# Splitting transposed head pairs in gapped half copies on VectorE, with the preparation of two pairs in a new order

## The chip, the cores and the metric

The kernel runs on one core of a Trainium2 chip. The metric is the device time of one execution in microseconds; the kernel before has a median of 217.63 us over 7 runs. Engines are named as in the profile: PE is TensorE, DVE is VectorE, ACT is ScalarE, POOL is GpSimd, SP is the queue that issues nearly all DMAs.

## The reference

Block-sparse attention for 4 batches of 8 heads, 768 positions, head width 64, followed by a gated block:

```python
scores = (1.0 / np.sqrt(D)) * np.matmul(q, k.transpose(0, 1, 3, 2))
scores = np.where(mask, scores, -1e9)           # mask: neighbours, first and last block, 3 drawn blocks of 32
attn = np.exp(scores - max); attn = attn / (attn.sum(-1) + 1e-9)
x = (attn @ v) with heads side by side           # (4, 768, 512)
h = np.maximum(x @ w_in, 0.0); u, v = h[..., :512], h[..., 512:]
v_n = (v - mean(v)) / np.sqrt(var(v) + 1e-6)     # over the last axis
v_s = einsum('ts,bsd->btd', w_spatial, v_n) + b_spatial[None, :, None]
out = (u * v_s) @ w_out
```

Inputs and output are float32; the kernel computes its products in bfloat16.

## The kernel before

The 32 heads are worked in 16 pairs, four pairs to a batch. A head's scores are computed with the keys on the partitions, in six chunks of 128 keys. For one chunk, `qk_exp` (L356) multiplies a chunk of k with all 768 queries (two products of 384 columns, L361), and ScalarE takes the exponential of the 128x768 result (L365). One such chunk is a *slot*; a pair takes 12 slots, s = 0 to 11, and g = 12p + s counts them through. The mask is part of the product: below the 64 rows of k and q stand 24 rows with block indicators and penalties. Seven slots later `av` (L370) multiplies the exponentials with v, which has a column of ones so that the row sums come along; `norm` (L436) divides (rc L442, xn L443), and `xtr` (L459) transposes the result of a pair by DMA into xt. The first batch (pairs 0 to 3) runs through the same steps in halves of 384 queries (`qk_exp_half` L386, `av_half` L405, `xtr_half` L427 with its evacuation L434), over 48 values of g.

For pairs 4 to 15, k and q come to their place in five steps: `load` (L105) issues three DMAs on SP (L110) into staging tiles with two buffers per name; `prepare` (L147) casts k, q and v to bfloat16 on GpSimd (L140 and L143); `tr_dma` (L342) transposes k and q of both heads by DMA (L344) into tt_k and tt_q, 128 partitions by six chunks of 128 columns; `split_pair` (L347) copies the upper and the lower 64 partitions of tt into the two heads' own tiles with two VectorE copies of 64x768 (L350), one call for k and one for q. The split of pair p + 1 has to be done before the slot s = 0 of that pair.

The gated block of a batch is a list of steps made by `moe_units` (L487), one product of 128x512 in each (L520), and the slots of the following batch take them from a queue, one a slot at first and about two later. A v part is evacuated by VectorE (vsb L533), followed by statistics (L536, L537); after each three v parts GpSimd computes rstd (L540, L542), and VectorE normalises (vn L547). The spatial products follow (gn L586), transposed by DMA on SP (gt L590), then the output products, evacuated by ScalarE (L608) or VectorE (L610). These products share two PSUM banks, `moe0` and `moe1`, one buffer each, so that a product can start only when the one before the last has been evacuated.

The order of everything is the order of the program text: each engine works through its own queue in that order. The slots at which `load`, `prepare`, `tr_dma` and `split_pair` are called are written out by hand in the loop over p and s from L728 on; what is called earlier in the text stands earlier in the queues of all engines that it uses.

Of the kernel before, what the change touches and what calls it, by code (L numbers as in the profile page):

```python
# [11 lines left out]
BF16 = mybir.dt.bfloat16  # L12
# [14 lines left out]
def kernel(  # L27
# [16 lines left out]
    nc = tc.nc  # L44

    B, H, S, D = q.shape
# [3 lines left out]
    NCH = S // 128  # L50
# [6 lines left out]
    NG = H // 2  # L57
# [282 lines left out]
    tt = {}  # L340

    def tr_dma(p, nm):  # L342
        tt[nm, p] = work.tile([128, NCH, 128], BF16, tag=f"tt_{nm}", bufs=2, name=f"tt_{nm}")
        nc.sync.dma_start_transpose(out=tt[nm, p],  # L344
                                    in_=nat.pop((nm, p)).rearrange("p c h d -> p (c h d)"))

    def split_pair(p, nm):  # L347
        src = tt.pop((nm, p)).rearrange("x c n -> x (c n)")
        for h in range(2):
            nc.vector.tensor_copy(out=(qt if nm == "q" else kt)[(2 * p + h) % H][0:D, :],  # L350
                                  in_=src[h * D:(h + 1) * D, :])


    a_ref, av_ref, xn_ref, xt_ref = {}, {}, {}, {}
# [317 lines left out]
    for g in range(N0):  # L672
        qk_exp_half(g)
        if g < 6:
            keep_warm(2)
        if g == 12:
            mask_product(1, bank([128, 512], FP32), dve_copy)
        if g == 0:
            qt_mask(1, 2, 0)
        if g == 1:  # L680
            tr_k_head(1, 0, NCH)
            cast_qk(1, "k", slice(0, 1), nc.vector)
            qt_mask(2, 4, 0)
        for p, third in tr_slots.get(g, ()):
            tr_pair(p, "k", third)
        if g in q_slots:
            tr_q_pair(*q_slots[g])
        if g == 13:
            for p in range(2):
                cast_q_pair(p, 1)  # L690
            qt_mask(4, 8, 1, nc.gpsimd)
            cast_q_pair(2, 1)
            cast_weights(2)
            cast_q_pair(3, 1)
            cast_weights(2)
            prepare(4, "kq")
            load_weights(3)
        if g in (6, 20):
            qt_mask(*{6: (4, 8, 0), 20: (1, 4, 1)}[g])
        if g == 26:  # L700
            moe_q.extend(moe_units(0))
        if g == 28:
            tr_dma(4, "k")
            tr_dma(4, "q")
            cast_weights(2)
            load(4, "v")
            load(5, "kqv")
            wspt(0)
            wspt(1)
            cast_weights(1)  # L710
            prepare(5, "kq")
            wspt(2)
            wspt(3)
            tr_dma(5, "k")
            tr_dma(5, "q")
            wspt(4)
            wspt(5)
            load(6)
        if g in (36, 42):
            cast_v(4 if g == 36 else 5)  # L720
        if g in (39, 45):
            split_pair(4, "k" if g == 39 else "q")
        first_batch_rest(g)
        if g >= 26 and g != 32:
            moe_q.popleft()()
        first_batch_x(g)

    for p in range(NG, NP + 1):  # L728
        for s in range(12):
            g = 12 * p + s  # L730
            change = NG < p < NP and p % NG == 0
            j, ci = divmod(g, NCH)
            if p == NP and g - LAG >= 2 * NP * NCH:
                break
            if p < NP:
                qk_exp(j, ci)
            if p + 1 < NP and s in ((3, 6) if p == NG else (7, 10)):
                split_pair(p + 1, "k" if s in (3, 7) else "q")
            if s == (10 if p == NG else 8 if change else 6) and p + 2 < NP:
                tr_dma(p + 2, "k")  # L740
                tr_dma(p + 2, "q")
            if s == (7 if p == NG else 1) and p + 2 < NP:
                prepare(p + 2)
                if p == 6:
                    cast_weights(2)
            if s == (9 if change else 7) and p + 2 < NP:
                if p + 3 < NP:
                    load(p + 3)
                if p == 5:
                    load_weights(2)  # L750
            if g < N0 + 11 and g != N0 + 8:
                moe_q.popleft()()
            if g == N0 + 11:
                slots_left = 49
            if moe_q and slots_left > 0:
                budget += len(moe_q) / slots_left
                slots_left -= 1
                while moe_q and budget >= 0.5:
                    moe_q.popleft()()
                    budget -= 1  # L760
            first_batch_rest(g)
            first_batch_x(g)
            if g >= N0 + LAG:
                ja, qc = divmod(g - LAG, NCH)
                av(ja, qc)
                if qc == NCH - 1:
                    norm(ja)
            if s == (6 if change else 8) and p > NG:
                xtr(p - 1)
            if s == 11 and change:  # L770
                moe_q.extend(moe_units(p // NG - 1))
                slots_left = 48 if p < NP - NG else 49
                budget = 0.0
# [34 lines left out]
```

## Time and profile before

| | |
|---|---|
| median of 7 runs | 217.63 us (216.16 to 219.61) |
| the profiled execution's own time | 217.57 us |
| its span | 215.8 us |
| TensorE busy | 206.1 us (95%) |
| ScalarE busy | 172.4 us (80%) |
| VectorE busy | 131.0 us (61%) |
| GpSimd busy | 69.6 us (32%) |
| TensorE clock granted, mean | 0.997 |

The profile is of one execution. Times in its views are microseconds from the span's start, durations of single instructions are nanoseconds in the list of groups and microseconds in the timeline. A line of the list of groups has the line of the kernel, the engine, the operation, what it writes and reads, the shapes and the count; then the busy time in all and the mean of one; then how long the engine stood idle just before these instructions, and what ended that. A line of the timeline has start, duration and the same names; in square brackets is the idle time ahead of it and what ended it. A line of the list of waits says who waited for whom, for how long in all, how often, and the longest.

### The profile page before, as it was taken

To read this page: it belongs to the slowest core of one execution; us is meant where nothing else is said; L and a number is where in the kernel's file an instruction comes from. 1 tells how busy PE (TensorE), PEld (TensorE's weight loads), DVE (VectorE), ACT (ScalarE), POOL (GpSimd) and SP (SyncE) were. 2 spreads that over 40 slices of the span, in tenths; PEclk is the share of its full clock that TensorE was granted. 3 is DMA by queue.
4 is the path that set the end of the run, shared out by engine and by line. 5 is a ranking of instruction groups with operands and counts; after the bars stand their busy time and mean duration, and the time that the engine had idled before them with its cause. 6 is when DMAs were issued, how large, how long until landed. Compare 5 with 4: busy or idle time off the path is not lost.

```text
span 215.8 us, 5234 instructions
## 1 busy us (share of the span) xinstructions
PE 206.1 (95%) x2065; PEld 125.9 (58%) x2099; DVE 131.0 (61%) x311; ACT 172.4 (80%) x238; POOL 69.6 (32%) x97
## 2 busy tenths in 40 slices
PE   8999999999979999999999999999899999999993
PEld 7667766566646666655566565655555655544441
DVE  6776949967554546356957464445978344585542
ACT  7799999999988999998899888888789885266031
POOL 7678979802626121403242400401502000022000
PEclk9999999999999999999999999999999999999998
DMA  6999999998999899999989138979702124620246
GB/s 175 282 328 382 392 346 281 211 140 260 269 254 265 135 242 181 269 293 309 189 206 255 40 71 228 259 166 303 151 12 39 24 52 87 220 101 0 59 119 235
DMA packets 64936, 42.24 MB, mean 196 GB/s; under 512 B 46896, under 2 KB 60560, under 8 KB 64912
## 3 DMA queue, kind: packets, MB, share of 16 engines
q1 hardware_dynamic: 64624, 41.58, 77.0%
q8 instruction: 16, 0.26, 0.5%
q10 hardware_dynamic: 288, 0.33, 0.5%
q14 instruction: 8, 0.07, 0.1%
HBM read 24.38 MB, written 6.29 MB: 142 GB/s over the span
## 4 chain that ended last, share of the span: by engine, by line
PE 75%; DMA 7%; DVE 5%; SPq 4%; POOL 3%; issue 3%; ACT 0%; POOLq 0%; ACTq 0%; DVEq 0%
PE ps_moe L520 30%; PE ps L361 17%; PE ps_av L377 11%; DMA st_v<-in_v_dram 6%; PE ps L396 6%; PE ps_av L412 3%; PE ps_t L520 3%; PE ps_sc L520 3%; SPq L110 1%; POOL vv L143 1%; SPq L472 1%; DVE kt_all L350 1%; DVE vsb L533 1%; DMA out_dram<-osb 1%; POOL rstd L542 1%
## 5 line engine op out<-in xcount | busy, mean ns | idle before, releaser
L365 ACT ACTIVATE a_all<-ps 128x768 bf16<-128x768 f32 x144 | 113.5, 813 | 15.9 <-PE ps L361 9.6
L361 PE MATMUL ps<-qt_all,kt_all 88*128 88x384 bf16 x288 | 70.3, 325 | 1.1 <-DVE qt_all L350 1.1
L377 PEld LDWEIGHTS <-a_all 128*128 128x128 bf16 x864 | 46.1, 97 | 34.0 <-issue 1.6
L377 PE MATMUL ps_av<-vv,a_all 128*128 128x65 bf16 x864 | 50.8, 194 | 0.3
L520 PE MATMUL ps_moe<-w_in_t,xt 128*128 128x512 bf16 x143 | 45.2, 378 | 1.8 <-DVE vsb L533 0.8
L400 ACT ACTIVATE a_all<-ps 128x768 bf16<-128x768 f32 x48 | 35.6, 812 | 2.8 <-PE ps L396 2.3
L140 POOL CAST nat_k<-st_k 128x768 bf16<-128x768 f32 (+1 forms) x14 | 11.1, 790 | 71.9 <-DMA st_k<-in_k_dram 62.5
L520 PE MATMUL ps_moe<-vn,w_spt 128*128 128x512 bf16 x110 | 33.1, 378 | 0.3
L586 DVE SCALAR_TENSOR_TENSOR gn<-ps_moe,b_col,un 128x512 bf16<-128x512 f32 x20 | 15.0, 749 | 21.4 <-PE ps_moe L520 17.9
L520 PEld LDWEIGHTS <-xt 128*128 128x128 bf16 x192 | 18.6, 97 | 15.1 <-issue 0.8
L396 PE MATMUL ps<-qt_all,kt_all 88*128 88x384 bf16 x96 | 23.6, 327 | 0.7 <-ACT a_all L400 0.2
L520 PE MATMUL ps_moe<-w_out_t,gt 128*128 128x512 bf16 x73 | 21.5, 378 | 0.3
L520 PEld LDWEIGHTS <-w_spt 128*128 128x128 bf16 x144 | 13.8, 97 | 11.6
L361 PEld LDWEIGHTS <-kt_all 88*128 88x128 bf16 x288 | 19.0, 98 | 1.6 <-DVE qt_all L350 1.2
L412 PEld LDWEIGHTS <-a_all 128*128 128x128 bf16 x288 | 14.9, 98 | 6.3 <-issue 0.9
L533 DVE TENSOR_SCALAR vsb<-ps_moe 128x512 bf16<-128x512 f32 x18 | 12.3, 682 | 10.0 <-PE ps_moe L520 9.8
L536 DVE BATCH_NORM_STATS2 stats<-vsb 128x6 f32<-128x512 bf16 x24 | 16.6, 693 | 1.5 <-ACT vsb L531 0.8
L412 PE MATMUL ps_av<-vv,a_all 128*128 128x65 bf16 x288 | 17.1, 194 | 0.4 <-DVE xt L434 0.4
L540 POOL TENSOR_SCALAR std<-mv 128x3 f32<-128x3 f32 x8 | 1.9, 244 | 43.1 <-DVE mv L537 30.6
L610 DVE COPY osb<-ps_moe 128x512 f32<-128x512 f32 x10 | 6.9, 690 | 13.3 <-PE ps_moe L520 9.8
L443 DVE TENSOR_TENSOR xn<-ps_av,rc 128x384 bf16<-128x384 f32 x24 | 13.4, 557 | 0.8
L520 PEld LDWEIGHTS <-gt 128*128 128x128 bf16 x96 | 8.8, 97 | 7.1
(100 smaller groups left out, 212.8 us busy)
## 6 DMA issues: line engine op xcount, KB each, us to landing
out_dram<-osb SPq DMA_DIRECT2D x23, 256.0 KB, 3.3
st_v<-in_v_dram SPq DMA_DIRECT2D x14, 384.0 KB, 5.3
st_k<-in_k_dram SPq DMA_DIRECT2D x13, 384.0 KB, 4.3
st_q<-in_q_dram SPq DMA_DIRECT2D x12, 384.0 KB, 3.6
wst<-in_moe_w_spatial_dram SPq DMA_DIRECT2D x3, 768.0 KB, 9.1
wst<-in_moe_w_in_dram SPq DMA_DIRECT2D x4, 512.0 KB, 7.5
wst<-in_moe_w_out_dram SPq DMA_DIRECT2D x2, 512.0 KB, 6.6
st_q<-in_q_dram SPq DMA_DIRECT2D x4, 192.0 KB, 6.1
```

The source lines that it names most:

```text
L140: eng.tensor_copy(out=dst, in_=src)
L361: nc.tensor.matmul(out=ps[:, hf * 512:hf * 512 + HALF], lhsT=kt[j % H][:, ci * 128:(ci + 1) * 128], rhs=qt[j % H][:, hf * HALF:(hf + 1) * ...
L365: nc.scalar.activation(out=a_ref[j][:, ci, :].rearrange("p (b c) -> p b c", b=2), in_=ps.rearrange("p (b c) -> p b c", b=2)[:, :, 0:HALF], ...
L377: nc.tensor.matmul(out=av_ref[j][:, qc, :], lhsT=a_ref[j][:, ci, qc * 128:(qc + 1) * 128], rhs=vv[p % NG][:, h, ci, :], start=(ci == 0), s ...
L396: nc.tensor.matmul(out=ps[:, u * 512:u * 512 + HALF], lhsT=kt[j][:, ci * 128:(ci + 1) * 128], rhs=qt[j][:, grp * HALF:(grp + 1) * HALF], s ...
L400: nc.scalar.activation(out=a_ref["half", gh][:, 2 * i:2 * i + 2, :], in_=ps.rearrange("p (b c) -> p b c", b=2)[:, :, 0:HALF], func=AF.Exp, ...
L412: nc.tensor.matmul(out=av_ref["half", gh][:, qc, :], lhsT=a_ref["half", gh][:, ci, qc * 128:(qc + 1) * 128], rhs=vv[p][:, h, ci, :], start ...
L443: nc.vector.tensor_tensor(out=xn_ref[p][:, :, h, :], in0=ps[:, :, 0:D], in1=rc.to_broadcast([128, NCH, D]), op=ALU.mult)
L520: nc.tensor.matmul(out=box[0], lhsT=lhs, rhs=rhs, start=(i == 0), stop=(i == n - 1))
L533: nc.vector.tensor_scalar(out=vsb[:, tcc, :], in0=ps, scalar1=0.0, scalar2=None, op0=ALU.max)
L536: nc.vector.bn_stats(out=stats, in_=vsb[:, tcc, :])
L586: nc.vector.scalar_tensor_tensor(out=gn[:, tcc, :], in0=ps, scalar=b_col[:, tcc:tcc + 1], in1=un[:, tcc, :], op0=ALU.add, op1=ALU.mult)
```

## The change

`tr_dma` makes tt with 144 columns per chunk and uses the first 128, so that the chunks lie 16 columns apart. `split_pair` copies three chunks at a time: each of its copies of 64x768 becomes two of 64x384, with a source of three pieces and a destination without gaps.

The slots change for some pairs. The v cast of pair 5 moves from g = 42 to p = 4, s = 5 (g = 53), the q split of pair 4 from g = 45 to g = 44. In the slots of pair 4, the load of pair 7 moves from s = 7 to s = 11, behind the transposes of pair 6. In those of pair 5, pair 6 is split at s = 6 and 8 instead of 7 and 10, pair 7 is prepared at s = 7 instead of 1 and transposed at s = 9 instead of 6, and the load of pair 8 with the last two weight loads moves from s = 7 to s = 10. In those of pair 7, the load of pair 10 moves from s = 7 to s = 10. Within a slot, `prepare` now stands ahead of `tr_dma`.

```diff
     def tr_dma(p, nm):
-        tt[nm, p] = work.tile([128, NCH, 128], BF16, tag=f"tt_{nm}", bufs=2, name=f"tt_{nm}")
+        tt[nm, p] = work.tile([128, NCH, 144], BF16, tag=f"tt_{nm}", bufs=2,
+                              name=f"tt_{nm}")[:, :, 0:128]
         nc.sync.dma_start_transpose(out=tt[nm, p],
                                     in_=nat.pop((nm, p)).rearrange("p c h d -> p (c h d)"))
 
     def split_pair(p, nm):
-        src = tt.pop((nm, p)).rearrange("x c n -> x (c n)")
+        src = tt.pop((nm, p))
         for h in range(2):
-            nc.vector.tensor_copy(out=(qt if nm == "q" else kt)[(2 * p + h) % H][0:D, :],
-                                  in_=src[h * D:(h + 1) * D, :])
+            dst = (qt if nm == "q" else kt)[(2 * p + h) % H]
+            for c in (0, 3):
+                nc.vector.tensor_copy(out=dst[0:D, c * 128:(c + 3) * 128],
+                                      in_=src[h * D:(h + 1) * D, c:c + 3, :])
...
-        if g in (36, 42):
-            cast_v(4 if g == 36 else 5)
-        if g in (39, 45):
+        if g == 36:
+            cast_v(4)
+        if g in (39, 44):
             split_pair(4, "k" if g == 39 else "q")
...
     for p in range(NG, NP + 1):
+        change = NG < p < NP and p % NG == 0
+        splits = {NG: (3, 6), NG + 1: (6, 8)}.get(p, (7, 10))
+        s_prep = {NG: 7, NG + 1: 7}.get(p, 1)
+        s_tr = {NG: 10, NG + 1: 9}.get(p, 8 if change else 6)
+        s_load = {NG: 11, NG + 1: 10, NG + 3: 10}.get(p, 9 if change else 7)
...
-            if p + 1 < NP and s in ((3, 6) if p == NG else (7, 10)):
-                split_pair(p + 1, "k" if s in (3, 7) else "q")
-            if s == (10 if p == NG else 8 if change else 6) and p + 2 < NP:
+            if p + 1 < NP and s in splits:
+                split_pair(p + 1, "k" if s == splits[0] else "q")
+            if p == NG and s == 5:
+                cast_v(5)
+            if s == s_prep and p + 2 < NP:
+                prepare(p + 2)
+                if p == NG + 2:
+                    cast_weights(2)
+            if s == s_tr and p + 2 < NP:
                 tr_dma(p + 2, "k")
                 tr_dma(p + 2, "q")
-            if s == (7 if p == NG else 1) and p + 2 < NP:
-                prepare(p + 2)
-                if p == 6:
-                    cast_weights(2)
-            if s == (9 if change else 7) and p + 2 < NP:
-                if p + 3 < NP:
-                    load(p + 3)
-                if p == 5:
+            if s == s_load and p + 3 < NP:
+                load(p + 3)
+                if p == NG + 1:
                     load_weights(2)
```

## The prediction, made before the change was run

> **What bounds the kernel now.** I read the page's first part, then the list of what TensorE waited for, then the timelines of VectorE and GpSimd around each such wait.
>
> ```profile
> PE 206.1 (95%) x2065; PEld 125.9 (58%) x2099; DVE 131.0 (61%) x311; ACT 172.4 (80%) x238; POOL 69.6 (32%) x97
> ```
>
> TensorE is busy for 206.1 of 215.8 us, and that work is untouched. Only its idle time can be recovered, and only a new wait of TensorE can be lost. VectorE has 85 us free in total, but it works in order: what matters is whether a copy stands ahead of something that TensorE needs. TensorE's waits from 36 to 66 us, then from 66 to 180 us (time in all, number, longest):
>
> ```profile
> PE ps L361 <- DVE qt_all L350: 1.1, 1, 1.1
> PE ps_av L412 <- DVE xt L434: 0.4, 1, 0.4
> PE ps_moe L520 <- DVE vsb L533: 0.3, 1, 0.3
> ...
> PE ps_moe L520 <- DVE vsb L533: 0.6, 1, 0.6
> PE ps_moe L520 <- DVE osb L610: 0.3, 1, 0.3
> ```
>
> That is 2.7 us of named waits over the stretch in which pairs are split. The largest is pair 6's first product, held by the q split. The VectorE timeline, then GpSimd's:
>
> ```profile
> 57.83 0.18 DVE L537 BATCH_NORM_AGGREGATE mv<-stats 128x2 f32<-128x6 f32 x1
> 60.78 0.41 DVE L547 TENSOR_SCALAR vn<-vsb,mv,rstd 128x512 bf16<-128x512 bf16 x1 [2.77 <-POOL rstd L542]
> 61.11 0.19 DVE L442 RECIPROCAL rc<-ps_av 128x6 f32<-128x6 f32 x1
> 61.34 0.56 DVE L443 TENSOR_TENSOR xn<-ps_av,rc 128x384 bf16<-128x384 f32 x1
> 61.81 0.73 DVE L350 COPY kt_all<-tt_k 64x768 bf16<-64x768 bf16 x2
> 62.56 0.74 DVE L547 TENSOR_SCALAR vn<-vsb,mv,rstd 128x512 bf16<-128x512 bf16 x2
> 63.21 0.73 DVE L350 COPY qt_all<-tt_q 64x768 bf16<-64x768 bf16 x2
> ...
> 57.42 0.83 POOL L140 CAST nat_q<-st_q 128x768 bf16<-128x768 f32 x1
> 58.62 0.83 POOL L143 CAST vv<-st_v 128x768 bf16<-128x768 f32 x1 [0.38 <-DMA st_v<-in_v_dram]
> 59.54 0.23 POOL L540 TENSOR_SCALAR std<-mv 128x3 f32<-128x3 f32 x1
> 59.86 0.89 POOL L542 TENSOR_TENSOR rstd<-std,mhalf 128x3 f32<-128x3 f32 x1
> ```
>
> VectorE has the statistics at 58.01, but pair 7's v cast is ahead of rstd in GpSimd's queue and waits for its load. So rstd ends at 60.75, VectorE stands for 2.77 us, and both splits of pair 6 come late. The second wait (0.37 us at 40.6) and the one near 153 us have another cause, a copy held by a cast:
>
> ```profile
> 29.27 8.79 POOL L183 CAST ws_nat<-wst 128x1536 bf16<-128x1536 f32 x3 [1.03 <-DMA wst<-in_moe_w_spatial_dram]
> ...
> 36.56 2.08 DVE L350 COPY kt_all<-tt_k 64x768 bf16<-64x768 bf16 x2
> ...
> 151.53 1.64 DVE L350 COPY kt_all<-tt_k 64x768 bf16<-64x768 bf16 x2
> ```
>
> The first of these copies ends with the cast at 38.06. The last falls on three casts that start at 150.46. Elsewhere two such copies take 0.71 to 0.74.
>
> **What the Trainium skill says.** "VectorE: DVE Perf Modes", section "What auto-detection actually checks": a copy uses two ports only if the outermost dimensions of source and destination are both even or equal. Three gapped chunks (3) into 384 adjacent columns (384) are neither, which leaves the one-port mode at two elements a cycle. The same page, "Side-by-side", gives some 150 cycles of fixed cost, 0.96 GHz, four elements a cycle at best. The trace agrees: 768/4/0.96 = 200 ns plus 155 is the median of 355 (the skill's 150 cycles are 156 ns). "SBUF — State Buffer", "Who interferes with whom": a two-port VectorE copy and a GpSimd instruction shut each other out, a one-port copy with one input contends with nothing. The 2.08 us above agree with the first half; no row shows the second.
>
> **The change, part by part.**
>
> *The copies.* Pairs 4 to 15 have 48 copies, busy 11.2 + 9.0 = 20.2 us. Undisturbed they would be 48 x 0.355 = 17.0, so 3.2 us are contention. Afterwards there are 96 of 64x384. The nearest row is a copy of that shape at two elements a cycle, from PSUM:
>
> ```profile
> L277 DVE COPY qt_all<-ps_moe 64x384 bf16<-64x384 bf16 x16 | 5.6, 349 | 1.1 <-PE ps_moe L307 0.8
> ```
>
> I take 0.355 from the formula (384/2/0.96 = 200 plus 155), near its 0.349. So 96 x 0.355 = 34.1 us, VectorE +13.9, to 145. A split of k or q becomes 1.42 instead of 0.72. Bounds: 0.255 if the mode stays at four, 0.555 at one element a cycle. Most of the 13.9 us fall beside other work, but what queues behind counts:
> - k of pair 4: 1.42 for 2.08. VectorE is 0.66 earlier at xt, and the wait of 0.37 goes: **-0.37**.
> - k of pair 14: 1.42 from 151.53 to 152.95, while the evacuation behind it started at 153.09: **-0.14** of 0.59; the rest stays.
> - pair 10 (104.4): both splits run back to back, 1.4 us more. The evacuation at 105.97 moves to 107.3 and ends by 108.0; the bank is wanted when the next product ends, at 108.4 (ScalarE takes that one at 108.42). The next one, 109.78 to 110.47, moves to about 111.4 and is wanted at 111.4 (ScalarE's at 111.43): 0 to 0.3, I take **+0.2**.
> - pair 9: k and q end at 94.5, the evacuation behind waits for its product until 94.66: nothing. Pair 13: 139.27 to 140.7, evacuation 0.65 later; a product of four steps at about two a slot is 1.8 us: nothing. Pairs 11 and 15: vn shifts by 0.7, its fourth tile is wanted over 0.7 later. Pairs 7, 8 and 12: gn comes up to 0.7 later, its bank is free for a product of six steps (over 2.5 us), and 0.8 us or more of idle time follow: nothing. Pair 5: the q split ends at 50.0, wanted at 52.25; the evacuation at 51.10 loses at most 0.1.
>
> *The order of pairs 6 and 7.* Pair 7's casts move six slots back, so rstd stands free: 58.01 plus 0.23 + 0.89 and gaps is 59.3 instead of 60.75. k of pair 6 moves ahead of vn and fills that gap. On the clock of before: k 58.01 to 59.43, vn to 59.84, rc and xn to 60.6, q to 62.0, vn twice to 62.8. TensorE asks for q at 62.55 (the end of 63.61 less 1.06): **-1.06**, with 0.5 to spare. The fifth vn tile is wanted at about 63.8, and pair 7's v cast may hold vn until 62.7: covered.
>
> *Queues.* Pair 7's load moves behind pair 6's transposes on SP, from 49.6 to about 56; three issues of 0.5 and some 4 us of flight bring the casts to 60.3 to 62.7. Its transposes then stand behind the transpose of xt, at about 62.1, and land by 67.4; the split is at 70.5. Pair 8's load and both w_out loads go from 60.1 to about 64.6. The casts of pair 8 come at 69.5 to 72, where its transposes stood at 70.85 anyway, by slot; w_out is cast by 75 and first used at 82. Pair 10's load passes an xt transpose and some gt transposes, from 83.9 to about 87; the casts end by 93.1, its transposes were at 93.09 and may slip by 1, its split is at 104.4. All this costs 0; were the cover gone, the slip itself would be paid, up to 1 us. Pair 5's v cast leaves rstd's way at 41.2, but vn came only at 48.85: 0. Moving the q split of pair 4 one slot earlier: 0 to 0.1 either way.
>
> *The gaps.* No trace shows a gapped tt. The nearest, w_spt, is written in pieces with a pitch: SP took at least 1277 ns to issue it, landing at least 2.9 us, median 4.8 in a crowded stage; tt has 1211 and 2.7. I take 0. A gain is not excluded, for the writes go elsewhere, but a deadline met earlier moves nothing. Two microseconds of delay at pair 5 (k landed at 46.6) would put its q split to 51.5 and the evacuation behind 0.4 late, and pair 6's q would end at 62.2: +0.5 at most.
>
> **Sum:** -1.06 - 0.37 - 0.14 + 0.2 = -1.37 on a profiled execution of 217.57 us (span 215.8 and 1.8 around it), which stands 0.06 under the median of 217.63: **216.2 us**, -0.65%. A measurement of this kernel can tell about 0.5% (1.1 us) from no change, so this lies just outside.
>
> **Rivals.**
> 1. *The copies keep the four-element mode.* 96 x 0.255 = 24.5 us: VectorE is hardly dearer, but casts still hold it. Then only the new order counts, -1.06, or 216.5. For it: nothing in this trace shows that odd counts decide. Against: the page's rule.
> 2. *One element a cycle* ends slower. At 0.555 a split is 2.2 us. At pair 6: 58.0 + 2.2 + 0.41 + 0.76 + 2.2 = 63.6 against 62.55, so 1.05 waited, nothing gained. Pair 10: evacuation 108.9 to 109.6 for 108.4, +1.2. Pair 9: copies until 96.1, osb to 96.8 for 95.4, +1.4. Pair 14: +0.6. With -0.37 lost too: +3.2, or 220.8. It decides from 58.01 + 8c + 1.17 = 62.55, c = 0.42 us a copy. Against: the row of 349 ns at two a cycle.
> 3. *A transposed pair or a load comes late* where I called it covered (pairs 5, 7, 8, 10): a wait of 0.5 to 1.5 takes the place of the one removed, 216.7 to 217.7. For it: SP and DMA are full in this stage. Against: at least 3 us between landing and split of pairs 7, 8 and 10.
>
> **Chances.** Forecast 0.58, the first rival 0.12, the second 0.14, the third 0.16. The forecast's own spread (0.5 either way for the copy costs, 0.6 for the median of some runs) puts about four fifths of it beyond -0.5%; half of rival 1 and a quarter of rival 3 add to that: faster 0.6. Slower is rival 2, some of rival 3 and the forecast's tail, 0.2; 0.2 is left between. The range, 214.7 to 218.8, takes in all but rival 2 and the tails.
>
> **What would show it.** VectorE near 145 us (135 for rival 1, 164 for rival 2); 96 copies at 0.34 to 0.36, with no outliers; rstd of the second half right after its statistics; no wait of L361 for L350 and none of L412 for xt. Wrong if copies differ from 0.355, if L361 still waits at pair 6, or if vsb waits grow past 1 us.

## The result: slower by about 1%

The changed kernel has a median of 220.54 us over 12 runs (217.57 to 222.16), the kernel before 217.79 over the 31 runs beside it. The ratio is 1.0096 with an interval of [1.0058, 1.0135]. The forecast was 216.2 us with a range up to 218.8, so both the sign and the range were wrong. One remark is needed to read the numbers below: in some executions of most kernels here the mean granted clock of TensorE falls from 1.000 to 0.992 or 0.984 and the time grows by some 2.5 to 3 us, and a ratio leaves out the executions over 1.5% above the fastest of their kernel, while a median has all. Of the twelve executions of the changed kernel ten have this fall; the other two took 217.57 and 218.10 us, about what the kernel before takes.

The profiled execution took 220.42 us, its span is 218.6 (before: 215.8). The page's first part, and its row for the granted clock:

```profile
PE 207.1 (95%) x2065; PEld 125.8 (58%) x2099; DVE 140.9 (64%) x359; ACT 172.3 (79%) x238; POOL 69.3 (32%) x97
...
PEclk9999999999999999996999999999999999999999
```

VectorE grew by 9.9 us, of which the copies are 8.7 (20.2 us before, 28.9 after). TensorE grew by 1.0 us though its work is the same: slice 19 of the clock row has a 6, so some of it ran slower. TensorE's waits from 36 to 66 us, and from 66 to 183 us:

```profile
PE ps_moe L525 <- DVE vsb L538: 0.3, 1, 0.3
...
PE ps_moe L525 <- DMA xt<-xn: 3.6, 1, 3.6
PE ps_moe L525 <- DVE osb L615: 0.3, 1, 0.3
PE ps_moe L525 <- DVE vsb L538: 0.2, 1, 0.2
```

The waits that the forecast removes are gone: no product waits for qt_all, none for xt's evacuation in the first batch, and the wait near 153 us has shrunk. In their place stands a wait of 3.6 us that the kernel before did not have at all. The list says it is for the DMA that writes xt. TensorE's timeline around it (start, duration, in brackets the idle time ahead and what ended it):

```profile
95.32 0.38 PE L525 MATMUL ps_moe<-w_in_t,xt 128*128 128x512 bf16 x1
99.32 0.39 PE L525 MATMUL ps_moe<-w_in_t,xt 128*128 128x512 bf16 x1 [3.63 <-DMA xt<-xn]
99.55 0.35 PE L382 MATMUL ps_av<-vv,a_all 128*128 128x65 bf16 x6
99.74 0.75 PE L366 MATMUL ps<-qt_all,kt_all 88*128 88x384 bf16 x2
```

These are the first products of batch 1's gated block, in the slots of pair 9. They multiply xt of pairs 4 to 7, and pair 7's piece is not there. After the wait a pair of score products takes 0.75 us where it takes 0.49 elsewhere. The busy times by stretch show why (PE, PEld, VectorE, ScalarE and GpSimd; after them stand the granted clock, the share of the DMA engines and GB/s):

```profile
94.00:99.30 5.30, 1.70 (x14) 0.76 (x12) 0.76 (x2) 1.68 (x3) 2.43 (x3) 1.00 1.12 322
99.30:104.00 4.70, 4.62 (x30) 2.49 (x32) 3.02 (x6) 1.81 (x3) 0.38 (x1) 0.64 1.03 280
```

The mean clock is 0.64 over the 4.7 us after the idle time. The trace's clock record has it at half from 99.83 to 103.24 and at full around that. Half of 3.41, 1.7 us, is lost on top of the wait. One such stretch in 218 us makes a mean clock of 0.992, two make 0.984.

Taking the start of the first exponential of each pair as a milestone, the 2.84 us of longer span fall apart like this: the start up to g = 24 is 0.55 shorter (an edit touches nothing there; other executions differ as much), g = 24 to pair 4 is 0.37 shorter, pair 5 to pair 6 is 1.06 shorter (11.36 to 10.30), pair 9 to pair 10 is **5.25 longer** (12.47 to 17.72), and pair 12 to pair 14 is 0.42 shorter (25.07 to 24.65). All the rest agrees within 0.02. So one stage, pair 9's, carries the whole loss: 3.6 us of wait and about 1.7 us of half clock.

### The profile page after: what moved, and what is told of

Same layout as the page of the kernel before. It is cut to its first block, busy times and chain, and to the rows that moved or that the text cites. A ratio compares the mean times of both kernels' runs of the same rounds, so it can differ in the third digit from the quotient of the medians.

```text
span 218.6 us, 5281 instructions
## 1 busy us (share of the span) xinstructions
PE 207.1 (95%) x2065; PEld 125.8 (58%) x2099; DVE 140.9 (64%) x359; ACT 172.3 (79%) x238; POOL 69.3 (32%) x97
## 4 chain that ended last, share of the span: by engine, by line
PE 84%; DMA 6%; DVE 4%; issue 2%; POOL 1%; SPq 1%; ACT 0%; ACTq 0%; DVEq 0%; POOLq 0%
PE ps_moe L525 33%; PE ps L366 21%; PE ps_av L382 12%; PE ps L401 6%; PE ps_av L417 4%; PE ps_t L525 3%; PE ps_sc L525 3%; DMA st_v<-in_v_dram 3%; DMA xt<-xn 2%; DVE vsb L538 1%; DMA out_dram<-osb 1%; PE ps_av L438 1%; DVE osb L615 1%; DVE kt_all L355 1%; DVE kt_all L277 1%
## 5 line engine op out<-in xcount | busy, mean ns | idle before, releaser
L525 PE MATMUL ps_moe<-w_in_t,xt 128*128 128x512 bf16 x143 | 46.1, 385 | 4.9 <-DMA xt<-xn 3.6
L355 DVE COPY kt_all<-tt_k 64x384 bf16<-64x384 bf16 x48 | 14.4, 339 | 0.6 <-DMA tt_k<-nat_k 0.5
L355 DVE COPY qt_all<-tt_q 64x384 bf16<-64x384 bf16 x48 | 14.5, 340 | 0.5
```

The lines of the kernel that those rows point to most:

```text
L355: nc.vector.tensor_copy(out=dst[0:D, c * 128:(c + 3) * 128], in_=src[h * D:(h + 1) * D, c:c + 3, :])
L525: nc.tensor.matmul(out=box[0], lhsT=lhs, rhs=rhs, start=(i == 0), stop=(i == n - 1))
```

## Why xt is late: SP's queue

The wait names a DMA, so the next view is SP's own timeline. Before first, then after:

```profile
88.29 3.20 SPq L611 DMA_DIRECT2D out_dram<-osb  x4
91.74 1.26 SPq L466 DMA_TRANSPOSE xt<-xn  x1
```

```profile
89.25 0.57 SPq L110 DMA_DIRECT2D st_q<-in_q_dram  x1
89.87 0.47 SPq L110 DMA_DIRECT2D st_k<-in_k_dram  x1
90.38 0.47 SPq L110 DMA_DIRECT2D st_v<-in_v_dram  x1
90.94 2.79 SPq L616 DMA_DIRECT2D out_dram<-osb  x4
93.83 2.14 SPq L471 DMA_TRANSPOSE xt<-xn  x1
```

Before, SP had come to this transpose at 91.49 and stood waiting for its data: VectorE finished xn of pair 7 at 91.72 and SP issued the transpose at 91.74. The data landed at 95.63 (the completions of its semaphore in the trace come from 95.56 to 95.63). The weight load that reads it started at 97.30 and the product, the second of this row, at 97.52:

```profile
97.30 0.60 PE L520 MATMUL ps_moe<-w_in_t,xt 128*128 128x512 bf16 x2
```

So the product had 1.9 us to spare, the weight load 1.7. (Some expectations below were written with 0.2 us, from a landing at 97.34. That figure adds 5.6 us to 91.74, which is the flight of the xt transpose issued at 86.81; this one flew for 3.9.) After, xn was finished at 89.73, earlier, because TensorE was earlier. But SP was still at pair 10's load until 90.85 and then issued four stores of batch 0's output until 93.73. The transpose left at 93.83, 4.1 us after its data was ready, and landed at 99.28; TensorE wanted it at 95.7. TensorE asks 1.8 us earlier, and the data lands 3.65 later (2.1 from the later issue, 1.55 from a longer flight, 5.45 us). Less the 1.9 to spare, that makes the 3.6 us.

SP is behind for a longer chain of reasons. From 68.2 us on, its rows leave hardly a gap. Pair 8's load and the weight loads begin at 64.19 instead of 60.09, the two gt transposes behind them end at 72.05 instead of 70.75, pair 8's own transposes start at 72.14 instead of 70.85 and the first takes 2.51 us to issue instead of 1.23, pair 9's load starts at 76.04 instead of 73.47, its transposes at 83.61 instead of 81.25. Pair 10's load, put later on purpose, then falls right ahead of the stores. That move adds nothing to what SP issues ahead of xt: before, the load stood ahead of it too, at 83.87. The sum over SP's rows from pair 6's first transpose (53.37 before, 53.48 after) to xt says where the lateness comes from. The issues take 29.3 us before and 34.8 after. Of the 5.5 us more, 1.5 are pair 7's load, which before stood ahead of these transposes, and 4.0 are issues that took longer. The gaps between issues shrink from 8.8 to 5.4 us and so take up 3.4 of them. The rest, 2 us, is how much later SP comes to xt.

## The experiments

The theories that the runs were made for: **A**, pair 8's later load makes xt late, by pushing everything behind it on SP (later: SP is late as a whole because of the changed slots); **B**, pair 10's load does, by standing just ahead of xt; **C**, xt had almost no time to spare, so that it is waited for whenever TensorE is earlier, and **N**, the same with an SP that does not come earlier with TensorE; **D**, the gapped transposes or the longer copies are at fault; **S**, the length of SP's queue, with the stores in it, sets when xt goes out, and **T**, the DMA engines are so full that xt lands as late whenever it is issued; **V**, the executions of *before* with a lowered clock come from an xt that lands just in time. Ratios are to runs of the kernel before that were made beside each run. A trace is of one execution; where that one is far from its kernel's median, the text says so.

### The two halves of the change

**c_copies**: before, with only the gapped tiles and the half copies.

```diff
-        tt[nm, p] = work.tile([128, NCH, 128], BF16, ...)
+        tt[nm, p] = work.tile([128, NCH, 144], BF16, ...)[:, :, 0:128]
...
+            for c in (0, 3):
+                nc.vector.tensor_copy(out=dst[0:D, c * 128:(c + 3) * 128],
+                                      in_=src[h * D:(h + 1) * D, c:c + 3, :])
```

> Only the gapped tiles and the half copies, all slots as before. Common to all theories: VectorE busy about 141 us, the wait of TensorE at 40.6 us for xt is gone, the one of 1.06 us for pair 6's q near 62 us stays (rstd is still behind pair 7's v cast). Theory A (pair 8's late load puts SP behind) and theory B (pair 10's load stands ahead of pair 7's xt): no wait for xt near 95 us, since neither load has moved; span about 215.3, time 0.2 to 0.3% under before. Theory C (pair 7's xt had almost no slack, so whatever makes TensorE earlier is waited for there): a wait of 0.2 to 0.5 us for the DMA of xt, time equal to before.

Ratio 1.004 [1.0001, 1.0079], median 220.31, span of the profile 216.1. There is no wait for the DMA of xt, against theory C. But the wait for pair 6's q, which was to stay as it was, grew from 1.1 to 2.3 us. VectorE's timeline shows how (the first line has the wait for the late rstd):

```profile
60.45 0.41 DVE L552 TENSOR_SCALAR vn<-vsb,mv,rstd 128x512 bf16<-128x512 bf16 x1 [3.48 <-POOL rstd L547]
...
61.48 1.22 DVE L355 COPY kt_all<-tt_k 64x384 bf16<-64x384 bf16 x4
...
63.37 1.24 DVE L355 COPY qt_all<-tt_q 64x384 bf16<-64x384 bf16 x4
```

rstd is late as it was before, both splits still stand behind it, and each is 0.5 longer. The longer copies need the new order of pair 6. The trace is of an execution of 217.89 us, well under the median: 15 of the 22 have a mean clock of 0.992 or less, and this one has 1.000.

**c_order**: the new slots with the tiles and copies of before.

```diff
+        splits = {NG: (3, 6), NG + 1: (6, 8)}.get(p, (7, 10))
+        s_prep = {NG: 7, NG + 1: 7}.get(p, 1)
+        s_tr = {NG: 10, NG + 1: 9}.get(p, 8 if change else 6)
+        s_load = {NG: 11, NG + 1: 10, NG + 3: 10}.get(p, 9 if change else 7)
```

> Only the new slots, with the contiguous tiles and whole copies of before. Theories A, B and C all expect the wait for pair 7's xt near 95 us, 2.5 to 3.6 us long, TensorE's clock lowered after it, and a time 0.8 to 1.3% over before: the copies have no part in the loss. If instead the gapped transposes or the longer VectorE work make the loss (theory D), there is no such wait here and the span is about 214.7.

Ratio 1.0115 [1.0076, 1.0154], median 220.95, span 216.6. The order alone brings the wait for xt: issued at 92.38, 2.1 us waited. The wait for q of pair 6 is gone. So the wait for xt comes with the slots and not with the copies; the copies alone lose time too, but at pair 6's q. The trace is of the fastest of 13 executions and its clock stays at 1.00; ten of the 13 have a mean clock of 0.992 or less.

### Which of the moved loads

**u_load10**: after, with pair 10's load back at s = 7.

```diff
-        s_load = {NG: 11, NG + 1: 10, NG + 3: 10}.get(p, 9 if change else 7)
+        s_load = {NG: 11, NG + 1: 10}.get(p, 9 if change else 7)
```

> The changed kernel with pair 10's load back at s = 7 of pair 7. Theory B: its three issues and 1.2 MB are then out before the stores and pair 7's xt; the wait for xt falls under 1 us, the clock stays at 1.0, span about 214. Theory A: the queue ahead of xt is as long as in the changed kernel, xt is still issued about 93.8 us, its flight is at most 1 us shorter; wait 2.5 us or more, span 217.5 to 218.6.

Ratio 1.0058 [1.0031, 1.0084], median 219.21. The trace is of the slowest of 22 executions (221.76 us), so the sizes of its waits are not typical. In it the wait for xt went and another DMA took its place: the load now stands ahead of gt of the last spatial product, which SP issues at 89.81, and the first output product waits 3.3 us for it (until 95.14). A stretch at half clock follows there too. xt itself left at 94.67, later than in the changed kernel: theory B fails.

**u_load8**: after, with pair 8's load and the weight loads back at s = 7.

```diff
+        s_load = {NG: 11, NG + 1: 7, NG + 3: 10}.get(p, 9 if change else 7)
```

> The changed kernel with pair 8's load and the two w_out loads back at s = 7 of pair 5. Theory A: pair 8's casts end by 67 us, SP no longer stands at its transposes until 72.1, pair 7's xt is issued by 91.5 us, the wait for it falls to 1.5 us or less, span about 215. Theory B: pair 10's load is still just ahead of the stores and xt; wait 2.5 us or more. Theory C: a wait of at least 0.5 us stays here whatever SP gains, because TensorE is 2 us earlier than before and pair 7's xt is not.

Ratio 1.0059 [1.0026, 1.0091], median 219.68. The trace is again of an execution well above the median (221.40 us). xt is issued at 94.25, not by 91.5, and 2.4 us are waited for it, and now pair 7's q is late by 1.5 us, since its transpose stands behind those loads (66.94, 3.42 us to issue). Neither A nor B holds alone. In both traces, undoing one move passes the lateness to another item of the same queue. Pair 7's load, the third that moved, was not put back alone.

**load10_after**: after, with pair 10's load behind pair 7's xt, and pair 10's casts and transposes moved back accordingly.

```diff
+        s_prep = {NG: 7, NG + 1: 7, NG + 4: 11, NG + 5: 3}.get(p, 1)
+        s_tr = {NG: 10, NG + 1: 9, NG + 4: 99}.get(p, 8 if change else 6)
+        s_load = {NG: 11, NG + 1: 10, NG + 3: 99}.get(p, 9 if change else 7)
...
+            if p == 8 and s == 7:
+                load(10)
+            if p == 9 and s == 1:
+                tr_dma(10, "k")
+                tr_dma(10, "q")
```

> The changed kernel with pair 10's load behind pair 7's xt in SP's queue (its casts and transposes are moved back to match). SP has 1.6 us less to issue ahead of xt and 1.2 MB less is in flight ahead of it. By the theory that SP's queue length sets the time of xt: issued about 92.2, landed by 96.5, the wait falls from 3.6 to 0.5 to 1.3 us, no lowered clock, span 215 to 215.8. If the wait stays over 2.5 us, neither the place of this load nor SP's length at this point is the cause.

Ratio 1.0024 [0.9996, 1.0053], median 219.38, span 217.8, over the span expected. xt left at 92.70 and nobody waited for it. Pair 10's q was then late by 1.9 us, at 108.58. The load was not the thing that could wait.

### The stores ahead of xt

**p_store**: after, with batch 0's six stores on GpSimd's queue.

```diff
-                nc.sync.dma_start(out=dst, in_=osb)
+                (nc.gpsimd if b == 0 else nc.sync).dma_start(out=dst, in_=osb)
```

> The changed kernel with the six output stores of the first batch issued from GpSimd's queue instead of SP's; their bytes and times of readiness are the same. Theory S (the length of SP's in-order queue sets when pair 7's xt goes out): without the four stores ahead, 2.8 us of issue, xt goes out about 91 us, the wait for it falls from 3.6 to about 1 us, no lowered clock, span about 214.5. Theory T (the 16 DMA engines are full and every transfer ends when the bytes ahead of it are through): xt is issued earlier but flies longer and lands again at 98 to 99; wait 2.5 us or more, span as the changed kernel.

Ratio 1.0157 [1.011, 1.0204], median 221.11, span 219.1. xt left SP's queue at 91.44 instead of 93.83, flew for 4.9 us, and the wait for it fell from 3.6 to 0.6: S holds, T falls. The kernel was slower still. GpSimd's timeline:

```profile
96.90 2.68 POOL L616 DMA_DIRECT2D out_dram<-osb  x5
107.27 0.83 POOL L140 CAST nat_k<-st_k 128x768 bf16<-128x768 f32 x1 [7.68 <-issue]
...
110.06 0.89 POOL L547 TENSOR_TENSOR rstd<-std,mhalf 128x3 f32<-128x3 f32 x1
```

Five stores had stood behind pair 10's casts and went out together. Pair 11's load, issued on SP at 98.05, shares the DMA engines with them and landed 8.0 us after its issue, where the loads of pair 11 took 3.7 to 5.3 in the changed kernel. The casts came at 107.27 instead of 103.62, rstd behind them, and TensorE waited 2.8 us for vsb, with a stretch at half clock behind it. That the stores made the load slow is read from this stretch and not tested alone.

**pe_xt**: after, with pair 7's xt transposed by TensorE, as the kernel does for the last pair.

```diff
-        if p == NP - 1:
+        if p in (7, NP - 1):
```

> The changed kernel with pair 7's xt transposed by TensorE into a PSUM bank and copied by VectorE (six small products, 0.6 us, and 0.55 us), without its DMA. Both theories: the wait for xt near 95 us is gone; what is left is at most 0.7 us for the bank. If SP and DMA are late as a whole, gt of the last spatial products is next in line (its transposes stand before the stores) and takes up to 1 us. Span 213.5 to 214.5, 1.2 us or more under the changed kernel without its lowered clock, 1% under before.

Ratio 0.9978 [0.9955, 1.0001], median 217.26, and no execution of 14 has a lowered clock (216.76 to 218.11); span 215.8. With xt off SP the loss is gone, but the gain of 1% that was expected does not come. The price is a wait of 1.3 us: the transposes want xn in the slot in which VectorE makes it.

**pe_xt_s7**: the same one slot later.

```diff
+            if s == (7 if p == 8 else 6 if change else 8) and p > NG:
```

> The changed kernel with pair 7's xt transposed by TensorE, one slot later than in the earlier run of that kind, so that its input has been normalised by then. The 1.3 us wait of the transposes for xn should be gone or under 0.3 us and nothing else changes: span 214.3 to 214.8, time 0.5 to 0.8% under before, no lowered clock. If the products rather pay for the bank, 0.7 us of it stays.

Ratio 0.9995 [0.9974, 1.0016], median 217.74, span 215.6. The wait for xn fell to 0.3, but an output product now waits 1.2 us for ScalarE to empty a bank that the transposes share. The cost of the transposes moved and stayed, and the expected 0.5 to 0.8% did not come.

**pe_xt_store**: pe_xt and p_store together.

```diff
+        if p in (7, NP - 1):
...
+                (nc.gpsimd if b == 0 else nc.sync).dma_start(out=dst, in_=osb)
```

> Both edits at once. If xt was the only thing that waited for SP in this stage, nothing is gained over the one with xt on TensorE; if a wait for gt stands in its place, it does not change either, because the stores stand behind gt. Span 213.5 to 214.5. Stores that stand in GpSimd's queue may hold pair 9's and 10's casts for up to 1 us, covered.

Ratio 1.0162 [1.0097, 1.0227], median 221.38, span 218.3, where 213.5 to 214.5 was expected: the 1.3 of pe_xt and 2.7 for vsb, as in p_store. Pair 11's q load took 7.3 us to land.

**b_pe_xt**: the edit of pe_xt on the kernel before.

```diff
-        if p == NP - 1:
+        if p in (7, NP - 1):
```

> The kernel before with pair 7's xt transposed by TensorE. Before, xt landed 0.2 us ahead of its use, so by both theories nothing is waited for there and this only costs: 0 to 0.7 us more, time 0 to 0.3% over before. If many executions of before do wait for xt (theory V: what the one trace shows is the good case), the median falls by 0.3% or more.

Ratio 1.007 [1.0041, 1.01], median 219.47, more than the 0.3% expected. Before has no wait for xt to remove, so only the price is left: 1.3 us of wait and 0.5 of transposes. (The trace is of the fastest of 14 executions, with a span of 215.9.) The edit is a remedy for the new order and no gain of its own.

### What the order of pair 6 brings alone

**b_rstd**: before, with only pair 7's v cast moved from s = 1 to s = 7, out of rstd's way.

```diff
-                prepare(p + 2)
+                prepare(p + 2, "kq" if p == 5 else "kqv")
...
+            if p == 5 and s == 7:
+                cast_v(7)
```

> The kernel before with one call moved: the v cast of pair 7 from s = 1 to s = 7 of pair 5, so that rstd no longer stands behind it on GpSimd. Every load and transpose keeps its place. Theory N (xt of pair 7 was next in line, 0.2 us behind the wait for pair 6's q, because SP runs without a pause and does not come earlier with TensorE): the 1.06 us wait is gone, pair 7's xt is still issued at 91 to 92 us and lands at 97, and TensorE waits 0.7 to 1.2 us for it; span as before within 0.3 us. Theory A (only the changed slots make SP late): no wait for xt, span 214.7.

The profile, of the fastest of 22 executions, shows what the forecast's first step says: VectorE's wait for rstd fell from 2.77 to 1.55 us (pair 7's k and q casts still stand ahead of it), the wait for q from 1.1 to 0.3, SP's queue came forward with it (xt at 91.23), nobody waits for xt, so that N fails; span 214.9 against 215.8. The timed ratio is 1.0004 [0.9969, 1.0039]: 10 of its 22 executions have a clock under 0.995, and the others a median of 217.5 against 217.7 for before. A gain of 0.9 us in one profile is not confirmed by the times.

**b_rstd_pe**: the same with gapped tiles and half copies, and xt of pair 7 by TensorE one slot later.

```diff
+                prepare(p + 2, "kq" if p == 5 else "kqv")
...
+            for c in (0, 3):
+                nc.vector.tensor_copy(out=dst[0:D, c * 128:(c + 3) * 128], ...)
...
+        if p in (7, NP - 1):
```

> The kernel before with pair 7's v cast moved behind rstd, the gapped tiles and half copies, and pair 7's xt on TensorE at s = 7: the gains of the change without its new slots for loads and transposes. Theory N: no wait for xt, none over 0.4 us near 62; span about 214.3, as the changed kernel with xt on TensorE. Theory A: the same. If the new slots do bring something of their own beyond rstd, this one is up to 0.5 us slower than the changed kernel with xt on TensorE, most likely at pair 6's q (the longer copies behind vn).

Ratio 1.0173 [1.0118, 1.0228], span 219.7 where 214.3 was expected. Pair 6's q is 2.2 us late, with a stretch at half clock behind it. Moving the v cast alone did not set rstd free here: pair 7's k and q casts still run ahead of it (57.44 to 59.04), VectorE waits 2.99 us for it, and both splits stand behind that wait. So the longer copies need more of the new order than the v cast; whether it is the later k and q casts, the new split slots (6 and 8) or both was not tested.

### xt ahead of the stores

**xt_first**: after, with batch 0's stores held back in the program text until pair 7's xt has been issued. It uses the queues and operations of the changed kernel; only their order on SP differs.

```diff
+    held = []
...
+                if b == 0 and held is not None:
+                    held.append((dst, osb))
+                    return
                 nc.sync.dma_start(out=dst, in_=osb)
...
+                if p == 8:
+                    for dst, osb in held:
+                        nc.sync.dma_start(out=dst, in_=osb)
+                    held = None
```

> The changed kernel with the first batch's output stores held back in SP's queue until pair 7's xt is out. If the place of xt in that queue is the cause: xt is issued by 91 us, flies under 4.5 us without 1 MB of stores ahead of it, the wait is under 0.5 us (3.6 in the changed kernel), no lowered clock, span 213.4 to 214.2, time 0.8% or more under before. If SP is late as a whole for other reasons (theory A), another wait of over 1 us stands in its place, for gt or for a later pair's q.

Ratio 0.9873 [0.9815, 0.9931], median 216.31 over 6 runs (215.65 to 217.63), span 214.4. It is faster than both kernels. SP's timeline at the same place:

```profile
90.94 1.21 SPq L471 DMA_TRANSPOSE xt<-xn  x1
92.25 2.62 SPq L788 DMA_DIRECT2D out_dram<-osb  x4
```

The transpose leaves at 90.94 instead of 93.83 and flies for 4.9 us, where under 4.5 was expected. In TensorE's list of waits from 66 us on, the line for xt is gone:

```profile
PE ps_moe L527 <- DVE vsb L540: 0.6, 2, 0.4
PE ps_moe L527 <- DVE osb L617: 0.3, 1, 0.3
```

The span is 4.2 us shorter than after and 1.4 shorter than before. None of the 6 runs has a clock under 0.995, while 22 of the 49 runs of before beside it do; the other 27 have a median of 217.74, and against these the gain is 0.7%, the cautious end of the interval.

**b_xt_first**: the same order of issues in the kernel before.

```diff
+                if b == 0 and held is not None:
+                    held.append((dst, osb))
+                    return
```

> The kernel before with the same order of stores and xt on SP. Its trace had xt landing 0.2 us ahead of its use, so a typical execution gains nothing: time within 0.2% of before. If a part of the executions of before wait there (theory V), fewer of them show a lowered clock and the median falls by 0.2 to 0.5%.

Ratio 0.9994 [0.9957, 1.0031], span 215.6. Nothing gained, and 7 of 22 executions still have the lowered clock: this run does not support V. b_pe_xt, with 1 of 14 beside 7 of 27 of before, leans the other way, on too few runs to decide. What lowers the clock in before's executions stays open. One count belongs here: the kernels with the new slots and xt in time or off SP (pe_xt, pe_xt_s7, xt_first, o_xt_first, no_gap) have it in 1 of 76 executions, before beside them in 46 of 135. So the new slots seem to remove what stalls these executions too; no trace of such an execution of before was taken.

**o_xt_first**: xt_first with the contiguous tiles and whole copies of before.

```diff
-        tt[nm, p] = work.tile([128, NCH, 144], BF16, ...)[:, :, 0:128]
+        tt[nm, p] = work.tile([128, NCH, 128], BF16, ...)
...
-            for c in (0, 3):
+            nc.vector.tensor_copy(out=(qt if nm == "q" else kt)[(2 * p + h) % H][0:D, :],
+                                  in_=src[h * D:(h + 1) * D, :])
```

> The same order of stores and xt, with the changed kernel's slots but the contiguous tiles and whole copies of before. The wait for xt is under 0.5 us as well; against the kernel with gapped copies it keeps the wait of 0.4 us at 41 us and part of the 0.6 near 153: span 0.4 to 0.9 us longer.

Ratio 0.9995 [0.9971, 1.0019], median 217.46, span 216.1. Once xt is in time, the gapped copies are worth 1.15 us of median (217.46 to 216.31, measured side by side), rather more than expected. Without them there are waits of 0.4 each for xt's evacuation in the first batch and for the DMA of xt, and the longest k copy takes 2184 ns.

**no_gap**: xt_first with half copies but 128 columns a chunk.

```diff
-        tt[nm, p] = work.tile([128, NCH, 144], BF16, ...)
+        tt[nm, p] = work.tile([128, NCH, 128], BF16, ...)
```

> xt_first with tiles of 128 columns instead of 144, so that three chunks are adjacent. If the gap sets the copies' mode, the 96 copies take about 0.25 us each instead of 0.34, except where a GpSimd cast holds them: a handful of 0.5 to 2 us, as in the kernel before, and the first waits of before come back (0.4 us at 41). If the mode follows from the 3 alone, they take 0.34 without outliers.

Ratio 0.9991 [0.9953, 1.003], median 218.66, span 216.4. The k copies, as duration of one in ns (least, median, most) in no_gap and then in xt_first:

```profile
L355 DVE COPY kt_all<-tt_k x48: 220/252/1762, 36.3 to 166.0; 64x384 bf16<-64x384 bf16 x48
```

```profile
L355 DVE COPY kt_all<-tt_k x48: 311/340/349, 36.1 to 164.2; 64x384 bf16<-64x384 bf16 x48
```

The program differs in the gap alone. Without it a copy is faster, 252 against 340 ns, but some are held for up to 1762; with it none takes over 349. The faster copy gives the slower kernel, by 2.35 us of median. In no_gap's trace TensorE waits 1.1 us for vsb near 154, behind four k copies that take 2.10 us beside three GpSimd casts, 0.4 for pair 7's q at 74.0, whose copies take 2.38 beside casts, and 0.4 for xt's evacuation at 41; of these xt_first has only one for vsb, of 0.2.

## Why the prediction was wrong, by its own steps

**The copies: right.** 0.355 us was forecast and 0.340 measured, with the 96 of them between 310 and 350 ns and no outlier. VectorE came to 140.9 instead of 145: copies in a row overlap a little, so that four take 1.19 to 1.25 us and not the forecast's 1.42, and all 96 are busy for 28.9 us instead of 34.1. The first rival (four elements a cycle, 0.255) and the second (one, 0.555) both fall. "VectorE: DVE Perf Modes", section "What auto-detection actually checks", in the Trainium skill says the rule goes by the outermost non-unit dimensions, and the 340 ns agree with that; no_gap adds that three chunks side by side behave as one row of 384, at 252 ns, so that the gap and not the count of three sets the mode. What "SBUF — State Buffer", section "Who interferes with whom", states, that a one-port copy with one input does not contend with GpSimd, is now borne out by a longest copy of 350 ns.

**The order of pair 6: right.** -1.06 was forecast for pair 5 to 6 and 1.06 measured. VectorE's timeline follows the forecast's sequence:

```profile
57.01 1.19 DVE L355 COPY kt_all<-tt_k 64x384 bf16<-64x384 bf16 x4
58.42 0.41 DVE L552 TENSOR_SCALAR vn<-vsb,mv,rstd 128x512 bf16<-128x512 bf16 x1 [0.22 <-POOL rstd L547]
...
59.45 1.24 DVE L355 COPY qt_all<-tt_q 64x384 bf16<-64x384 bf16 x4
60.70 1.84 DVE L552 TENSOR_SCALAR vn<-vsb,mv,rstd 128x512 bf16<-128x512 bf16 x2
```

k fills the gap ahead of rstd, and q follows. Even the vn held by pair 7's cast (1.84 for two) came as forecast and cost nothing.

**Pairs 4, 10 and 14.** -0.37 was forecast and measured at pair 4. At pair 14 the gain was 0.42 instead of 0.14, because the split took 1.22 and not 1.42: the wait that was to stay in part went almost wholly. At pair 10 +0.2 was taken and nothing came (pair 10 to 12: 24.15 before, 24.14 after). The sum of these steps with what was measured is -1.06 - 0.37 - 0.42 = -1.85, better than the -1.37 forecast. xt_first shows the same three gains, but gives 0.9 of them back, 0.27 at pair 9 and 0.63 at pair 10, where TensorE waits 0.44 for vsb: without the stall ahead of it, pair 10 does cost something. Its span, 1.4 us under before, has 0.4 of that from the start, which no edit touches, so it meets the forecast's -1.37 partly by luck.

**Queues: "All this costs 0" is the step that failed.** It followed each moved load to the casts, transposes and split of its own pair, and found those covered. That part was right: no split was late. But it put at nothing, without pricing it, what a later SP does to everything else in the queue. It named what pair 10's load would pass, "an xt transpose and some gt transposes", and asked only what that does to pair 10, and not what stands *behind* on SP: four stores and pair 7's xt. Instead of 0 the runs show xt issued 2.1 us later and landing 3.65 later, a wait of 3.6 us and 1.7 us of half clock, +5.25 us in pair 9's stage. That the stores ahead of xt are part of it is shown by xt_first: with xt ahead of them the wait is gone and the span 4.2 us shorter. The times were off as well. Pair 10's load came at 89.25 instead of about 87, since SP was already 2.4 us behind with pair 9's transposes; the forecast had held pair 8's transposes at 70.85 "by slot", and they started at 72.14 because the queue ahead of them was longer. The last omission is the question of what is late next when the stall at pair 6 goes. xt of pair 7 landed 1.7 us ahead of its weight load in before, and the forecast's own first step, with TensorE 1.06 and 0.37 us earlier, spends most of that.

**Rival 3** was the nearest, with a transposed transfer that comes late. It named the wrong ones (the pairs' own, and pairs 5, 7, 8, 10) and priced it at 0.5 to 1.5 us. The stage lost 5.25, because three things add up: TensorE 1.8 us earlier, the data 3.65 later with 1.9 to spare, and a clock that falls after the wait. Its chance of 0.16 was too small for a queue that SP's timeline of before shows without a gap over 0.25 us for 20 us (69.47 to 89.86).

**The gaps: right.** Gapped transposes of q take SP 1240 ns at the median and land 2.8 us after the issue at best, as contiguous ones do in before (1240 ns and 2.7 us). Their median landing is 3.7 in after, but that goes with the slots: 3.5 in c_order with contiguous tiles, 2.8 in b_rstd_pe with gapped ones.

## What to carry to other kernels

When an issue is moved on an in-order queue, list what stands behind its new place and how much time each of those items has before its use; the moved item's own deadlines are only half of it. When a stall goes, look for the transfers that the stall had been covering: one with 1.7 us to spare is the next stall when the product comes 1.8 us earlier. Take each transfer's own landing for this; two transposes of the same kind, issued 5 us apart, flew for 5.6 and 3.9 us here. Where a queue is full, order it by due time (here: the store that nobody waits for goes behind the transpose that TensorE needs) before moving work to another engine: the two tried here, TensorE and GpSimd, each passed on a price of its own.

## What was not expected of the hardware

- **A long wait of TensorE costs more than its length, and whether it does depends on where it lies.** In all 18 traces the granted clock changes in steps of 3.41 us: the stretches at full clock are whole multiples of it (95.57 us is 28 of them, 61.44 is 18, 109.23 is 32), and each stretch at half clock ahead of the last products is one, which costs half of it, 1.7 us. Cut into these periods from its first full stretch on, a trace has the clock at half after every period in which TensorE stood idle for 2.24 us or more (2.24 in b_rstd_pe, 2.45 in u_load8, 2.84 in p_store, 2.91 in the changed kernel, 3.28 in u_load10), and after none with 1.91 us or less. Two waits of one length show it, 2.24 us in b_rstd_pe and 2.25 in c_copies. The first lies within one period and leaves PE 1.17 busy us of 3.41; the second lies across two, with 1.69 and 2.82, and the clock stays. The rows are b_rstd_pe's, then c_copies':

```profile
61.67:65.08 3.41, 1.17 (x14) 0.59 (x12) 3.27 (x11) 1.16 (x3) 0.00 (x0) 1.00 0.91 269
65.08:68.49 3.41, 3.41 (x27) 1.89 (x26) 1.50 (x3) 1.91 (x3) 2.43 (x3) 0.50 0.90 296
...
59.76:63.17 3.41, 1.69 (x20) 1.00 (x17) 2.65 (x9) 2.41 (x4) 0.66 (x1) 1.00 0.82 213
63.17:66.58 3.41, 2.82 (x30) 1.74 (x31) 2.81 (x8) 1.92 (x3) 1.60 (x2) 1.00 0.99 262
66.58:69.99 3.41, 3.35 (x41) 2.13 (x39) 0.75 (x1) 3.07 (x5) 1.27 (x2) 1.00 1.42 277
```

  "TensorE: Matmul & The Clock Gate", section "HAM oscillation — how this bites in real kernels", in the Trainium skill gives as an abstract rule no gaps over some 3.4 us; here 2.24 us within one period were enough, and the measurement decides.
- **Issues on SP sometimes stretch.** A transpose that takes 1.2 us to issue elsewhere took 2.14 (xt in the changed kernel), 2.51 (pair 8's k) and 3.42 (pair 7's q in u_load8), so a full queue gets later than its items' usual durations add up to. What holds them is not shown: the DMA engines' share was 0.97, 1.41 and 1.20 during these, and up to 1.17 during transposes of 1.2 to 1.3 us.
- **A slower copy can be the better one.** 340 ns without contention gave a kernel 2.35 us faster than 252 ns with outliers of 1762.
